# A layer-norm, attention and MLP kernel: a new prologue, transposes by DMA, and logits of two units in three steps from a pool of PSUM banks

## The chip, the cores and the metric

One core of one Trainium2 chip. The metric is the device time of one execution in microseconds (us). Engines: PE multiplies matrices, DVE and ACT do element-wise work and empty PE's results out of PSUM, POOL masks, and SP issues all loads, stores and DMA transposes from one queue, in order. PSUM has eight banks of 128 x 512 float32 values. A matmul writes to a bank, and the bank is free for the next matmul when DVE or ACT has copied the result out (its *eviction*).

## The reference

x is 2048 x 1024. It is normalised to xn. Two branches are computed of xn and added to x.

```python
def _A_ref(x, wq, wk, wv, wo, beta):          # H = 32 heads of Dh = 32, N = 4 segments of L = 512
    q, k, v = ...                             # x @ wq, x @ wk, x @ wv, split into heads and segments
    phi = lambda t: jnp.where(t > 0, t + 1.0, jnp.exp(t))
    for s in range(N):
        p = softmax(qs @ ks.T * scale + causal_mask)
        a_dot = p @ vs
        pq = phi(qs)
        a_mem = (pq @ M) / (pq @ z + 1e-06)
        outs.append(g * a_mem + (1.0 - g) * a_dot)
        pk = phi(ks)
        M = M + pk.T @ vs;  z = z + pk.sum(...)
    return o @ wo

def _B_ref(x, w1, b1, w2, b2):                # w1: 2048 x 3584, w2: 3584 x 2048, mixing over the sequence
    u = gelu(layernorm(x).T @ w1 + b1)
    return (u @ w2 + b2).T

xn = layernorm(x)
return x + _A_ref(xn, ...) + _B_ref(xn, ...)
```

## The kernel before

It has four stages: a *head* (load x, statistics, xn and h, transposes of xn); the *hidden* matmuls h x w1; *attention*, into which the matmuls of w2 and wo (here: *main*) are strewn so that PE has work while others finish; and a short *tail*. Attention goes by *units*. A unit is four heads in one segment; there are 32, eight to a segment. Before the change each job has its fixed banks: logits 0 to 3, the projections 0 to 3 in between, weighing 4 and 5, main 6 and 7 in turn.

```python
LOGIT_STEPS = [[0], [1], [2, 3]]                       # blocks of 128 keys
def logits(self, u, step):                             # banks 0 to 3, one exp for the four
    ...
    fw.op("act", ...activation(self.pT[:, :, off:off + total], self.ps[:, 0:4, 0:total], ACT.Exp, scale=SCALE), ...)

def proj_v(self, m, c, b):                             # values of one 128-row block
    ...                                                # 8 matmuls into bank b
    fw.op("dve", ...tensor_copy(self.vA[i][:, c, :, 0:D_HEAD], self.bank(b)...), ...)

def k_transpose(self, u, b):                           # on PE, then exp (ACT) and phi (DVE)
    for c in range(4):
        fw.tp(bb[:, c * P:(c + 1) * P], self.kT[k][:, c * P:(c + 1) * P], self.ident[:])
    ...
    self.phi(self.pk[j][:]..., self.R_pk[j], bb, self.R_bank[b], 1)

def weigh(self, u, qb):                                # p @ v, phi(q) @ M, and the update of M
    ...                                                # matmuls into bank 4 + qb % 2
    fw.op("dve", ...tensor_copy(dst, self.ps[:, b, 0:n * VW]), ...)            # -> ost
    ...                                                # qb == 3: M update on DVE -> MZ32, MZbf

def combine(self, u):                                  # all on DVE: sums, reciprocal, gate, product, add
    ...
    fw.op("dve", ...tensor_tensor(self.prod[:], ost..., rec..., op=ALU.mult), ...)
    fw.op("dve", ...tensor_tensor(os[:], pv[:, :, 0, :], pv[:, :, 1, :], op=ALU.add), ...)

def main_emit(self, n):                                # n matmuls of main
    ...
    if end == total:                                   # a finished tile: DVE adds it to stg
        fw.op("dve", ...scalar_tensor_tensor(dst, self.bank(b), self.b2c[:, c:c + 1], dst, ...), ...)
        self.main_bank = 13 - b                        # 6, 7, 6, 7, ...

for u in range(N_UNIT):
    n0, n1, n2 = (10, 8, 6) if s == 0 else (11, 9, 9)
    ...
    self.logits(u, 0)
    if u: self.combine(u - 1)
    self.main_emit(n0)
    self.logits(u, 1);  self.main_emit(n1)
    self.logits(u, 2);  self.main_emit(n2)
    self.weigh(u, 0);   self.weigh(u, 1)
    self.proj_q(un, 0)                                 # un = u + 2
    self.o_transpose(u - 1, 2)
    self.k_transpose(u + 1, 3)
    self.weigh(u, 2)
    self.proj_k(un, 1)
    self.weigh(u, 3)
    self.proj_v(m, u % 4, 2)
    self.main_emit(n3)
```

Each engine does its work in the order in which these calls issue it. In the profiles the tiles have the program's names: ps_all is PSUM, qT and kT a unit's queries and keys, pT the logits after exp, vA the values, ost what weighing gives, stg rows of the output to which main is added, w2h a piece of w2, pkT phi(k) before and pk after its transpose.

The softmax here doesn't subtract the row's maximum and nothing guards it: scores larger than these inputs give would overflow.

Of the kernel before, what the change touches and what calls it, by code (L numbers as in the profile page):

```python
# [15 lines left out]
N_SEG = 4  # L16
# [14 lines left out]
PT_OFF = [0, 512, 896, 1152]  # L31
PT_COLS = 1280
# [69 lines left out]
class FW:  # L102
    N_DMA_SEMS = 64
    N_OUT_SEMS = 40
# [94 lines left out]
    def dma(self, out_ap, in_ap, reads=(), writes=(), is_output=False, issuer="sp", extra=(),  # L199
            record_reads=True):  # L200
# [9 lines left out]
        ins = es.eng.dma_start(out_ap, in_ap)  # L210
# [124 lines left out]
class _Kernel:  # L335
    SB_BASE = 16512
    SB_END = 229344
    LEAD = 2
    N_EARLY = 3
# [7 lines left out]
    def build(self):  # L347
        nc, ctx = self.nc, self.ctx
        self.fw = FW(nc, ctx)
        self.x_d = self.A_x[0].rearrange("(c p) d -> p c d", p=P)  # L350
        self.out_d = self.out[0].rearrange("(c p) d -> p c d", p=P)
        self.ps = ctx.enter_context(nc.psum_tensor("ps_all", [P, 8, 512], F32))
        self.R_bank = [Res(f"bank{b}", bank=b) for b in range(8)]
        self.alloc()
        block = ctx.enter_context(nc.Block())

        @block.sync
        def _(sp_eng):
            self.consts()
            self.norm_and_first_hidden()  # L360
            self.over_early()
            self.hidden()
            self.over_late()
            self.attention_and_out()
            self.fw.final_waits()


    def alloc(self):
        nc = self.nc
        a = self.keep = _Arena(nc, self.SB_BASE, self.SB_END)  # L370
        self.ident = a.take("ident", [P, P], BF16)
        self.brow1 = a.take("brow1", [N_FCH, P], BF16)
        self.brow2 = a.take("brow2", [N_TCH, P], BF16)
        self.b1c = a.take("b1c", [P, N_FCH], F32)
        self.b2c = a.take("b2c", [P, N_TCH], F32)
# [7 lines left out]
        self.ln_rs = a.take("ln_rs", [P, N_TCH, 2], F32)  # L383
        self.ln_nb = a.take("ln_nb", [P, N_TCH, 2], F32)
# [5 lines left out]
        self.gT = a.take("gT", [P, N_FCH, D_MODEL], BF16)  # L390

        self.R_ident, self.R_beta, self.R_gcol, self.R_gate = Res("ident"), Res("beta"), Res("gcol"), Res("gate")
        self.R_brow1, self.R_brow2, self.R_b1c, self.R_b2c = Res("brow1"), Res("brow2"), Res("b1c"), Res("b2c")
        self.R_eps, self.R_diag = Res("eps8"), Res("diag")
        self.R_st = [Res(f"st{c}") for c in range(N_TCH)]
        self.R_rs = [Res(f"rs{c}") for c in range(N_TCH)]
        self.R_vA = [[Res(f"vA{i}_{c}") for c in range(4)] for i in range(2)]
# [13 lines left out]
        self.w1ring = [e.take(f"w1s{i}", [P, N_TCH, 256], BF16) for i in range(3)]  # L411
        self.late_end = e.at
        self.R_xin = [Res(f"xin{c}") for c in range(N_TCH)]
        self.R_xnt = [Res(f"xnt{i}") for i in range(4)]
        self.R_h = [Res(f"h{c}") for c in range(N_TCH)]
        self.R_w1s = [Res(f"w1s{i}") for i in range(3)]

    def over_early(self):
# [6 lines left out]
        self.w2r = [e.take(f"w2h{i}", [P, 14, P], BF16) for i in range(4)]  # L425
# [5 lines left out]
        self.R_w2 = [Res(f"w2_{i}", wait) for i in range(4)]  # L431
# [8 lines left out]
        for c in self.mlp_order:  # L440
            for hf in range(2):
                rows = self.B_w2[hf * 14 * P:(hf + 1) * 14 * P, c * P:(c + 1) * P]
                self.w2_ring.srcs.append(rows.rearrange("(fc p) t -> p fc t", p=P))
        for bv in range(2):
            fw.dma(self.wv_sb[:, :, bv * 512:(bv + 1) * 512],
                   self.A_wv[:, bv * 512:(bv + 1) * 512].rearrange("(dc p) j -> p dc j", p=P), writes=[self.R_wv[bv]])
        self.wq_ring.ensure(0)
        self.wk_ring.ensure(0)

    def over_late(self):  # L450
# [5 lines left out]
        self.pk = [e.take(f"pk{i}", [P, 4, P], BF16) for i in range(2)]  # L456
        self.pT = e.take("pT", [P, 4, PT_COLS], BF16)
        self.ost = [e.take(f"ost{i}", [P, 32, VW], BF16) for i in range(2)]
        self.o_s = [e.take(f"o_s{i}", [P, 4, P], BF16) for i in range(2)]
        self.etmp = [e.take(f"etmp{i}", [P, SEG_L], BF16) for i in range(2)]  # L460
        self.mtmp = [e.take(f"mtmp{i}", [P, SEG_L], BF16) for i in range(2)]
# [11 lines left out]
        self.R_pk = [R(f"pk{i}") for i in range(2)]  # L473
        self.R_pTu = [R(f"pTu{k}") for k in range(4)]
        self.R_pTd = [R(f"pTd{k}") for k in range(4)]
        self.R_ost = [[R(f"ost{i}_{qb}") for qb in range(4)] for i in range(2)]
        self.R_os = [R(f"o_s{i}") for i in range(2)]
        self.R_etmp = [R(f"etmp{i}") for i in range(2)]
        self.R_mtmp = [R(f"mtmp{i}") for i in range(2)]
# [11 lines left out]
    def bank_bf(self, b):  # L491
        return self.ps[:, b, :].bitcast(BF16)


    def consts(self):
        fw = self.fw
        self.load_x(0, 1)
        self.load_x(1, 1)
        fw.dma(self.beta_sb[:], self.A_beta.partition_broadcast(P), writes=[self.R_beta])
        self.load_x(2, 2)  # L500
        self.w1_ring = _Ring(fw, [t[:] for t in self.w1ring], self.R_w1s, depth=2)
        for fp in range(N_FCH // 2):
            self.w1_ring.srcs.append(self.B_w1[:, fp * 256:(fp + 1) * 256].rearrange("(c p) f -> p c f", p=P))
        self.w1_ring.depth = 0
        self.w1_ring.ensure(0)
        self.load_x(4, 4)
        fw.dma(self.brow1[:], self.B_b1.rearrange("(c q) -> c q", q=P), writes=[self.R_brow1])
        fw.dma(self.brow2[:], self.B_b2.rearrange("(c q) -> c q", q=P), writes=[self.R_brow2])
        self.w1_ring.ensure(1)
        self.load_x(8, 4)  # L510
        self.load_x(12, 4)
        self.w1_ring.depth = 2

        fw.op("pool", lambda e: e.memset(self.ident[:], 0.0), writes=[self.R_ident])
        fw.op("pool", lambda e: e.affine_select(self.ident[:], self.ident[:], pattern=[[-1, P]],
                                                compare_op=ALU.not_equal, fill=1.0, base=0,
                                                channel_multiplier=1),
              reads=[self.R_ident], writes=[self.R_ident])

        fw.op("act", lambda e: e.activation(self.gcol[:], self.beta_sb[:], ACT.Sigmoid),  # L520
              reads=[self.R_beta], writes=[self.R_gcol])
# [4 lines left out]

    def late_consts(self):
        fw = self.fw
        fw.op("pool", lambda e: e.memset(self.eps8[:, 0, :], 0.0), writes=[self.R_eps])
# [5 lines left out]
        for i in range(2):  # L535
            fw.op("pool", lambda e: e.memset(self.vA[i][:], 1.0), writes=self.R_vA[i])
        gv = self.gcol[:].rearrange("p (g r) -> p g r", r=4)
# [4 lines left out]
        for row, R_row, col, R_col, n, b in ((self.brow1, self.R_brow1, self.b1c, self.R_b1c, N_FCH, 6),  # L542
                                             (self.brow2, self.R_brow2, self.b2c, self.R_b2c, N_TCH, 7)):
            with fw.group(reads=[R_row, self.R_ident], writes=[self.R_bank[b]]):
                fw.tp(self.bank_bf(b)[:, 0:n], row[0:n, :], self.ident[0:n, 0:n])
            fw.op("dve", lambda e: e.tensor_copy(col[:], self.bank_bf(b)[:, 0:n]),
                  reads=[self.R_bank[b]], writes=[R_col])


    def norm_and_first_hidden(self):  # L550
        fw = self.fw
        n_pair = N_TCH // 2
        for p in range(n_pair + 2):
            if p < n_pair:
                self.ln_stats(2 * p)
                self.ln_stats(2 * p + 1)
                self.ln_small(2 * p)
            if 1 <= p <= n_pair:
                self.ln_bias(2 * p - 2)
                for c in (2 * p - 2, 2 * p - 1):  # L560
                    self.ln_apply(c)
            if p == 1:
                self.late_consts()
            if p >= 2:
                for c in (2 * p - 4, 2 * p - 3):
                    self.x_transpose(c)
                    self.early_hidden(c)
            if p == n_pair - 1:
                self.w1_ring.ensure(0)

    def ln_stats(self, c):
        fw = self.fw
        src, st, R = self.xin[:, c, :], self.ln_st[:, c, :], self.R_st[c]
        fw.op("dve", lambda e: e.bn_stats(st[:, 0:6], src[:, 0:512]), reads=[self.R_xin[c]], writes=[R])  # L574
        fw.op("dve", lambda e: e.bn_stats(st[:, 6:12], src[:, 512:1024]), reads=[self.R_xin[c], R], writes=[R])  # L575
        fw.op("dve", lambda e: e.bn_aggr(self.ln_mv[:, c, :], st.rearrange("p (a s) -> p a s", s=6)),  # L576
              reads=[R], writes=[R])

    def ln_small(self, c):

        fw = self.fw
        R, Q = [self.R_st[c], self.R_st[c + 1]], [self.R_rs[c], self.R_rs[c + 1]]
        var, rs = self.ln_mv[:, c:c + 2, 1:2], self.ln_rs[:, c:c + 2, :]
        fw.op("dve", lambda e: e.tensor_scalar(rs[:, :, 0:1], var, LN_EPS, None, op0=ALU.add), reads=R, writes=Q)  # L584
        fw.op("dve", lambda e: e.tensor_scalar(rs[:, :, 1:2], var, 1.0 + LN_EPS, LN_EPS * LN_EPS,
# [167 lines left out]
    def weigh(self, u, qb):  # L753
# [12 lines left out]
        if upd:  # L766
            reads += [self.R_pk[u % 2]]
# [231 lines left out]
```

## Time and profile before

743.61 us is the median of three runs (743.41 to 745.54). The profiled execution took 742.3 us.

| stage, from the timeline of PE; the tail starts at the first matmul of the last output rows | us |
|---|---|
| first hidden matmul | 18.86 |
| head done | 50.5 |
| hidden done | 223.6 |
| first logits | 239.51 |
| one unit in segments 1 and 2 | 16.06 |
| tail starts | 721.33 |
| end | 742.3 |

The page's busy line and its chain of waits (the work that ended last, followed back through what released it):

```profile
span 742.3 us, 11641 instructions
...
PE 707.3 (95%) x5058; PEld 342.0 (46%) x5154; DVE 277.1 (37%) x617; ACT 280.4 (38%) x301; POOL 112.5 (15%) x154
...
PE 91%; DVE 4%; issue 1%; SPq 1%; ACT 1%; DMA 1%; POOL 0%; POOLq 0%; DVEq 0%
```

The waits of PE: on the left what PE was about to write, on the right whose work it waited for; the columns are us in total, times, longest:

```profile
PE ps_all L194 <- DMA brow_50<-in_B_b_dram: 15.0, 1, 15.0
PE ps_all L188 <- issue: 3.8, 11, 2.2
PE ps_all L188 <- DVE pk_1680 L673: 1.7, 1, 1.7
```

PE is the limit nearly everywhere: 95% busy, 91% of the chain. Its only long wait is 15.0 us at the very start, for a load of a bias; the next are 3.8 and 1.7. 50 matmuls of 128x512 take 10.79 us, 0.216 us each.

The timeline of PE over one unit of segment 1; the columns are start, duration, operation, and the number of instructions grouped:

```profile
401.15 0.40 PE L188 MATMUL ps_all<-qT_1673,kT_1676 32*128 32x512 bf16 x4
...
403.96 0.34 PE L188 MATMUL ps_all<-qT_1673,kT_1676 32*128 32x384 bf16 x4
...
406.28 0.34 PE L188 MATMUL ps_all<-qT_1673,kT_1676 32*128 32x256 bf16 x8
...
410.65 0.39 PE L194 MATMUL ps_all<-ident,o_s_1685 128*128 128x128 bf16 x4
410.88 0.39 PE L194 MATMUL ps_all<-ident,kT_1674 128*128 128x128 bf16 x4
...
417.22 0.40 PE L188 MATMUL ps_all<-qT_1671,kT_1674 32*128 32x512 bf16 x4
```

The three logit steps are at 401.15, 403.96 and 406.28, and the next unit's first at 417.22. The two lines of `ident` are the eight transposes on PE. Four of them occupy 0.22 us of the stream (410.655 to 410.878). No row carries an idle time in brackets: the unit has no gap.

### The profile page before, as it was taken

Reading aid. Unit: us, or ns where it says so; the run is one execution under the profiler, and the core shown is the slowest. Engines: PE = TensorE matmul, PEld = TensorE weight load, DVE = VectorE, ACT = ScalarE, POOL = GpSimd, SP = SyncE. Lnnn points to the kernel's source line nnn. Section 1 sums busy time; section 2 is a strip of 40 time slices with the busy share of each in tenths; the row PEclk is TensorE's granted clock in tenths of the full one; section 3 lists DMA queues with packets and bytes.
Section 4 is the critical chain, followed back from the end, with each engine's and each line's share of the span. In section 5 each row is a group of like instructions: output and inputs, shape, how many; then the busy total and the mean of one; then the engine's idle time right before and its main releaser. Section 6 shows DMA issues by size and latency. Waiting matters only on the chain.

```text
span 742.3 us, 11641 instructions
## 1 busy us (share of the span) xinstructions
PE 707.3 (95%) x5058; PEld 342.0 (46%) x5154; DVE 277.1 (37%) x617; ACT 280.4 (38%) x301; POOL 112.5 (15%) x154
## 2 busy tenths in 40 slices
PE   0999999999999999999999999999999999999996
PEld 0444444444444454454444455444455444444452
DVE  6930000000002234335454555554545554444543
ACT  2682121211212443544444343344444344443540
POOL 3640000000000221221121211121211112211220
PEclk9999999999999999999999999999999999999999
DMA  9429322323508141641615415052451606425003
GB/s 253 145 83 218 97 57 82 88 57 91 97 1 223 29 107 29 136 103 34 135 38 100 103 34 135 1 136 55 81 108 29 135 16 120 89 47 108 15 13 115
DMA packets 164603, 65.77 MB, mean 89 GB/s; under 512 B 125642, under 2 KB 156362, under 8 KB 164554
## 3 DMA queue, kind: packets, MB, share of 16 engines
q1 hardware_dynamic: 164554, 65.04, 37.5%
q8 instruction: 40, 0.66, 0.4%
q14 instruction: 9, 0.07, 0.0%
HBM read 59.79 MB, written 5.24 MB: 88 GB/s over the span
## 4 chain that ended last, share of the span: by engine, by line
PE 91%; DVE 4%; issue 1%; SPq 1%; ACT 1%; DMA 1%; POOL 0%; POOLq 0%; DVEq 0%
PE ps_all L188 89%; PE ps_all L194 2%; DVE ln_st L575 1%; SPq L210 1%; DVE ln_st L574 1%; DMA brow_51<-in_B_b_dram 1%; ACT pT L743 0%; DVE ln_mv L576 0%; POOL pT L749 0%; DVE xn_tmp_76 L607 0%; DVE ln_rs L584 0%; DVE fin_8030 L966 0%; DVE fin_8029 L966 0%; ACT xn_tmp_75 L604 0%; DVE xn_tmp_74 L607 0%
## 5 line engine op out<-in xcount | busy, mean ns | idle before, releaser
L743 ACT ACTIVATE pT<-ps_all 128x1536 bf16<-128x1536 f32 (+1 forms) x96 | 152.9, 1593 | 192.9 <-PE ps_all L188 192.9
L749 POOL TENSOR_SCALAR_AFFINE_SELECT pT<-pT 128x512 bf16<-128x512 bf16 x128 | 87.0, 692 | 585.1 <-ACT pT L743 585.1
L662 ACT ACTIVATE gT<-ps_all,b1c 128x512 bf16<-128x512 f32 x56 | 37.8, 689 | 134.5 <-PE ps_all L188 134.5
L710 DVE CAST vA_63<-ps_all 128x512 bf16<-128x512 f32 x16 | 11.1, 694 | 187.9 <-PE ps_all L188 187.7
L188 PE MATMUL ps_all<-h,w1s_79 128*128 128x512 bf16 x311 | 72.0, 382 | 2.7 <-issue 2.2
L188 PE MATMUL ps_all<-h,w1s_80 128*128 128x512 bf16 x314 | 72.3, 381 | 0.3
L188 PE MATMUL ps_all<-h,w1s_81 128*128 128x512 bf16 x251 | 55.6, 379 | 0.3
L188 PE MATMUL ps_all<-gT,w2h_663 128*128 128x512 bf16 x213 | 52.9, 380 | 1.1 <-issue 0.8
L188 PE MATMUL ps_all<-gT,w2h_662 128*128 128x512 bf16 x219 | 53.6, 381 | 0.3
L188 PE MATMUL ps_all<-gT,w2h_665 128*128 128x512 bf16 x214 | 53.0, 380 | 0.9 <-issue 0.6
L188 PE MATMUL ps_all<-gT,w2h_664 128*128 128x512 bf16 x218 | 53.3, 381 | 0.4 <-issue 0.2
L783 DVE CAST ost_1683<-ps_all 128x264 bf16<-128x264 f32 (+1 forms) x64 | 23.7, 391 | 71.8 <-PE ps_all L188 71.8
L783 DVE CAST ost_1684<-ps_all 128x264 bf16<-128x264 f32 (+1 forms) x64 | 23.7, 391 | 68.2 <-PE ps_all L188 68.1
L188 PEld LDWEIGHTS ps_all<-h,w1s_80 128*128 128x128 bf16 x320 | 31.4, 98 | 38.1 <-issue 0.6
L188 PEld LDWEIGHTS ps_all<-h,w1s_79 128*128 128x128 bf16 x320 | 30.7, 98 | 36.8 <-issue 3.0
L188 PEld LDWEIGHTS ps_all<-h,w1s_81 128*128 128x128 bf16 x256 | 25.0, 98 | 30.2
L188 PE MATMUL ps_all<-wo_sb,oT_1691 128*128 128x512 bf16 x126 | 32.4, 379 | 0.2
L188 PEld LDWEIGHTS ps_all<-gT,w2h_665 128*128 128x128 bf16 x224 | 20.6, 98 | 25.2 <-issue 2.5
L188 PEld LDWEIGHTS ps_all<-gT,w2h_663 128*128 128x128 bf16 x224 | 20.6, 98 | 25.2 <-issue 2.5
L188 PE MATMUL ps_all<-wo_sb,xnT_68 128*128 128x512 bf16 x127 | 30.5, 379 | 0.7 <-ACT xnT_68 L835 0.7
L188 PEld LDWEIGHTS ps_all<-gT,w2h_662 128*128 128x128 bf16 x224 | 19.3, 98 | 25.3 <-issue 6.4
L188 PEld LDWEIGHTS ps_all<-gT,w2h_664 128*128 128x128 bf16 x224 | 19.3, 98 | 25.3 <-issue 6.4
(167 smaller groups left out, 870.0 us busy)
## 6 DMA issues: line engine op xcount, KB each, us to landing
w1s_79<-in_B_w_dram SPq DMA_DIRECT2D x5, 1024.0 KB, 5.4
w1s_80<-in_B_w_dram SPq DMA_DIRECT2D x5, 1024.0 KB, 6.0
w1s_81<-in_B_w_dram SPq DMA_DIRECT2D x4, 1024.0 KB, 5.8
wq_658<-in_A_wq_dram SPq DMA_DIRECT2D x16, 256.0 KB, 3.0
wq_659<-in_A_wq_dram SPq DMA_DIRECT2D x16, 256.0 KB, 6.9
wk_660<-in_A_wk_dram SPq DMA_DIRECT2D x16, 256.0 KB, 2.9
wk_661<-in_A_wk_dram SPq DMA_DIRECT2D x16, 256.0 KB, 4.8
w2h_662<-in_B_w_dram SPq DMA_DIRECT2D x8, 448.0 KB, 4.9
```

The lines of the kernel that those rows point to most:

```text
L188: ins = self.nc.tensor.matmul(*args, **kwargs)
L194: ins = self.nc.tensor.transpose(out, in_, ident)
L210: ins = es.eng.dma_start(out_ap, in_ap)
L574: fw.op("dve", lambda e: e.bn_stats(st[:, 0:6], src[:, 0:512]), reads=[self.R_xin[c]], writes=[R])
L575: fw.op("dve", lambda e: e.bn_stats(st[:, 6:12], src[:, 512:1024]), reads=[self.R_xin[c], R], writes=[R])
L662: fw.op("act", lambda e: e.activation(self.gT[:, fc, half * 512:(half + 1) * 512], self.bank(b), ACT.Gelu_apprx_tanh, bias=self.b1c[:, fc: ...
L710: fw.op("dve", lambda e: e.tensor_copy(self.vA[i][:, c, :, 0:D_HEAD], self.bank(b).rearrange("p (h d) -> p h d", d=D_HEAD)), reads=[self.R ...
L743: fw.op("act", lambda e: e.activation(self.pT[:, :, off:off + total], self.ps[:, 0:4, 0:total], ACT.Exp, scale=SCALE), reads=self.R_bank[0:4],
L749: fw.op("pool", lambda e: e.affine_select(d, d, pattern=[[0, 4], [1, P]], compare_op=ALU.is_ge, fill=0.0, base=0, channel_multiplier=-1), ...
L783: fw.op("dve", lambda e: e.tensor_copy(dst, self.ps[:, b, 0:n * VW]), reads=[self.R_bank[b]], writes=[self.R_ost[o][qb]])
```

## The change

The intent was to take work off PE. Three parts:

- a prologue that makes h (which the hidden matmuls need) first, and starts PE with it;
- the transposes of xn, phi(k) and the attention output by DMA, not by PE;
- logits for *pairs* of units in three *windows* of 7, 7 and 6 banks, not in six steps of 4. Every job takes its banks from one pool and gives them back after eviction. Main holds one bank nearly always, so a window of seven needs all the others.

With that the whole order of a pair was written anew. The diff, cut to its core:

```diff
+    def take_bank(self):
+        return self.free.popleft()
+    def give_bank(self, b):
+        self.free.append(b)
...
-    def k_transpose(self, u, b):
-        ...fw.tp(...) on PE...
+    def pk_transpose(self, u):
+        self.fw.dma(self.pk[u % 3][:], self.pkT[:], ..., transpose=True)
...
-    def o_transpose(self, u, b):
-        ...fw.tp(...) on PE, ACT copy...
+    def o_transpose(self, u):
+        self.fw.dma(self.oT[s % 2][:, g, :]..., self.o_s[o][:]..., transpose=True)
...
+    EXPS = ((0, 1, 2, 3, 4, 5, 6), (7, 8, 9, 10, 11, 12, 13), (4, 5, 2, 3, 6, 7))
+    def window(self, p, w):
+        bank = {slot: self.take_bank() for slot in self.EXPS[w]}
+        ...
+        for slot, b in bank.items():
+            fw.op("act", ...activation(pT[:, slot, :], self.bank(b), ACT.Exp, scale=SCALE), ...)
+            self.give_bank(b)
...
+    def settle(self):                     # main is never near the end of its tile at a window
+        left = self.main_left()
+        if 0 < left < 12:
+            self.main_emit(left + 2)
+        elif self.main_at == 0:
+            self.main_emit(2)
...
+        for p in range(N_UNIT // 2):
+            a, b = 2 * p, 2 * p + 1
+            self.settle()
+            self.window(p, 0)
+            self.main_emit(5)
+            self.proj_q(a + 2)            # q copy on ACT, then exp (ACT) and phi (DVE)
+            self.main_emit(4)
+            self.proj_k(a + 2)            # kT cast on DVE, then exp (ACT) and phi (DVE)
+            if p: self.o_transpose(a - 1)
+            self.main_emit(9 if s == 0 else 16)
+            self.pk_transpose(a + 2)
+            self.settle()
+            self.window(p, 1)
+            self.main_emit(5)
+            self.proj_v(a)
+            self.main_emit(5)
+            for qb in range(4): self.weigh(a, qb)
+            self.combine(a)
+            self.main_emit(10 if s == 0 else 17)
+            self.settle()
+            self.window(p, 2)
+            self.o_transpose(a)
+            self.proj_q(b + 2)
+            self.proj_k(b + 2)
+            self.main_emit(4)
+            for qb in range(4): self.weigh(b, qb)
+            self.combine(b)               # before the value projection, and before the next window
+            self.proj_v(b)
+            self.pk_transpose(b + 2)
+            self.main_emit(goal - self.main_done)
```

## The prediction

Written before the changed kernel had run, with its code at hand but no time and no trace of it:

> **What bounds it now.** PE. The page has PE busy 707 of 742 us, and the chain of waits is 91% PE. In the timeline 50 matmuls of 128x512 take 10.79 us: 0.216 us each; there are 2816 (608 us). By stage: first hidden matmul at 18.9 us, head done at 50.5, hidden done at 223.6, units 14.2 us each in segment 0 and 16.06 in segments 1 and 2, last matmul about 735.9, end 742.3.
>
> **What it saves.**
> - Head: h first (stats 1.6 us after the landing at 3.45, h 0.55): PE starts near 6.5 us. Landings and stats gate chunks 1 and 2 (near 12.8); then eight matmuls a chunk, no transposes: done near 37 us with 32 matmuls more. About 20 us.
> - Transposes off PE: 0.22 us per four; 24 of k and 32 of the output: 12 us. The Trainium skill ("VectorE: DVE Perf Modes", The three transpose paths) gives 1309 ns for 128x128 by DMA; no run here shows it yet.
> - Logits: six steps a pair take 2.5 us, about 0.2 us of each switching; three windows about 2.0. 8 us.
> - Tail: eight serial DVE adds (0.6 each) become overlapped: 3 us.
>
> **What it adds: a new wait.** Main holds one bank, so a pair's first window needs all seven others, and PE waits for the eviction of proj_v(b), which stands on DVE behind combine(b), weigh(b)'s four casts, both phis and the kT cast. From the end of window 3, segments 1 and 2, with the trace's durations: ACT does six exps (pitch 0.485) and the q copy to 3.6, exp q to 4.3; DVE phi q to 5.3, kT to 6.0; ACT exp k to 6.7; DVE phi k to 7.7, casts to 9.1, M update to 9.8, combine (0.24+0.38+0.23+1.26+0.5) to 12.4, v cast to 13.1. PE has 20 matmuls, weigh(b) and proj_v: 7.5 us. It waits about 5.7 us. The same sum gives 2 us a pair in segment 0 (short combine, no phi q) and 3.6 in segment 3 with proj_v: about 63 us over 15 boundaries. The second window needs the just finished main bank (eviction 0.75 us, behind two matmuls): 0.6 x 16 = 10 us.
>
> So such a pair takes about 37 us, not 32.1.
>
> **Sum** (estimate): 742 - 20 - 12 - 8 - 3 + 63 + 10 = 772. With DVE idle at the end of proj_k the main wait is still about 3 us, giving about 740. Against that, the skill ("TensorE: Matmul & The Clock Gate", Part 1) says about 3.4 us of idleness can halve PE's clock; this trace agrees at the start (first hidden matmuls about 0.42 us apart, later 0.216).
>
> **Prediction: 766 us, 80% range 726 to 792. Faster by over 2%: 0.14; within 2%: 0.22; slower: 0.64.**
>
> **What would show it.** First hidden matmul near 6.5 us, head done near 37, hidden near 203. No matmuls of ident. Largest of PE's waits: logits behind the DVE cast of vA, 4 to 6 us each in segments 1 and 2; PE busy under 92%. A second, 0.6 us, behind the DVE add of stg. Few waits on transposes.
>
> **What would make it wrong.** A shorter DVE chain; DMA transposes slow enough to hold up the w1, w2, wq, wk loads behind them in the one queue (slower still); a head limited by loading.

## The result, and the profile after

787.56 us is the median of four runs (787.02 to 789.53); the kernel before took 743.53 us beside them. The ratio is 1.059, with a 95% interval of 1.0571 to 1.0608: slower by 6%. (A ratio is the mean time of one kernel's runs over that of the other's runs of the same rounds, so it is not quite the ratio of the medians quoted.) The profiled execution took 787.8 us.

The page's busy line and its chain of waits:

```profile
span 787.8 us, 11445 instructions
...
PE 707.0 (90%) x4728; PEld 333.6 (42%) x4808; DVE 272.4 (35%) x595; ACT 268.4 (34%) x492; POOL 114.0 (14%) x236
...
PE 75%; DVE 14%; ACT 9%; issue 1%; DMA 1%; POOL 0%; SPq 0%; ACTq 0%; POOLq 0%; DVEq 0%
```

The waits of PE:

```profile
PE ps_all L186 <- DVE vA L778: 52.5, 14, 5.0
PE ps_all L186 <- DVE stg L970: 6.6, 16, 0.4
PE ps_all L186 <- POOL pT L832: 6.0, 4, 2.6
...
PE ps_all L186 <- DVE ost L867: 1.6, 1, 1.6
```

PE fell from 95% to 90%, and the chain from 91% PE to 75%, with DVE at 14% and ACT at 9%. The new waits are named: 52.5 us for the DVE cast of vA in 14 places, then 6.6 for stg and 6.0 for POOL's masks. The 15.0 us at the start are gone.

The timeline of PE, the windows of a pair of segment 1; the bracket is the idle time before the row and who ended it:

```profile
414.05 1.00 PE L186 MATMUL ps_all<-qT,kT 32*128 32x512 bf16 x10 [4.97 <-DVE vA L778]
414.98 2.31 PE L186 MATMUL ps_all<-gT,w2h 128*128 128x512 bf16 x5
...
427.18 0.61 PE L186 MATMUL ps_all<-qT,kT 32*128 32x256 bf16 x12 [0.42 <-DVE stg L970]
...
438.79 0.61 PE L186 MATMUL ps_all<-qT,kT 32*128 32x384 bf16 x10
...
452.01 1.03 PE L186 MATMUL ps_all<-qT,kT 32*128 32x512 bf16 x10 [4.96 <-DVE vA L778]
```

Both pairs shown start with 4.96 us of idleness. (Segments 1 and 2 have eight pairs; the first starts with 3.31 us, the other seven with 4.96 to 4.97.) The pair takes 37.96 us (414.05 to 452.01), where two units took 32.13 before. There is a second, quieter loss. The ten logit matmuls behind the gap took 1.00 us and the five main matmuls 2.31. Where no long gap went before, ten take 0.61 (the row at 438.79) and five 1.25: PE comes back at half its rate. The profile has the granted clock (the share of PE's full clock that the chip's throttle let through) at 0.964 over the whole span; it was 1.000 before.

What PE waits for, from the chain of waits of the changed kernel between 400 and 416 us; start, duration, engine and tile:

```profile
401.49 3.04 ACT pT L824 x6
...
405.05 0.64 ACT etmp L717
...
406.04 0.69 DVE pqT L720
406.73 0.61 DVE kT L752
...
407.37 0.64 ACT etmp L717
...
408.36 0.69 DVE pkT L720
409.05 1.36 DVE ost L867 x4
...
411.70 1.24 DVE prod L906
...
412.96 0.42 DVE o_s L910
413.38 0.62 DVE vA L778
...
414.05 1.97 PE ps_all L186 x12
```

This is one string of work, each item waiting for the one above: six exps on ACT, exp of q and k on ACT with phi(q), kT and phi(k) on DVE between them, the four casts of weigh(b), then combine(b), and only then the cast of vA. That cast empties the last of the seven banks which the next window needs.

| stage | before | after | difference |
|---|---|---|---|
| start to first logits | 239.5 | 218.8 | -20.7 |
| attention | 481.8 | 549.3 | +67.5 |
| tail | 21.0 | 19.7 | -1.3 |
| span | 742.3 | 787.8 | +45.5 |

(The changed kernel has done four matmuls of main, 0.9 us, before its first logits; the kernel before has done none.)

So the prologue gave what it promised. Attention lost three times as much.

### The profile page after: what moved, and what is told of

The parts are those of the page before. It is cut to its first block, busy times and chain, and to the rows that moved or that the text cites. A ratio compares the mean times of both kernels' runs of the same rounds, so it can differ in the third digit from the quotient of the medians.

```text
span 787.8 us, 11445 instructions
## 1 busy us (share of the span) xinstructions
PE 707.0 (90%) x4728; PEld 333.6 (42%) x4808; DVE 272.4 (35%) x595; ACT 268.4 (34%) x492; POOL 114.0 (14%) x236
## 2 busy tenths in 40 slices
DMA packets 211181, 77.32 MB, mean 98 GB/s; under 512 B 173754, under 2 KB 203450, under 8 KB 211130
## 4 chain that ended last, share of the span: by engine, by line
PE 75%; DVE 14%; ACT 9%; issue 1%; DMA 1%; POOL 0%; SPq 0%; ACTq 0%; POOLq 0%; DVEq 0%
PE ps_all L186 75%; ACT pT L824 6%; DVE ost L867 2%; ACT etmp L717 2%; DVE prod L906 2%; DVE stg L970 2%; DVE kT L752 1%; DVE vA L778 1%; DVE pqT L720 1%; DVE pkT L720 1%; DVE etmp L718 1%; ACT qT L738 1%; DVE o_s L910 1%; DMA xin<-in_A_x_dram 1%; DVE srec L904 0%
## 5 line engine op out<-in xcount | busy, mean ns | idle before, releaser
L824 ACT ACTIVATE pT<-ps_all 128x512 bf16<-128x512 f32 x320 | 161.8, 619 | 298.5 <-PE ps_all L186 298.5
L186 PE MATMUL ps_all<-gT,w2h 128*128 128x512 bf16 x863 | 220.1, 392 | 1.8 <-issue 0.2
L186 PE MATMUL ps_all<-h,w1all 128*128 128x512 bf16 x878 | 195.7, 383 | 3.8 <-DVE h L603 2.8
L832 POOL TENSOR_SCALAR_AFFINE_SELECT pT<-pT 128x256 bf16<-128x256 bf16 (+3 forms) x176 | 89.0, 510 | 641.4 <-ACT pT L824 636.5
L186 PEld LDWEIGHTS ps_all<-h,w1all 128*128 128x128 bf16 x896 | 88.1, 98 | 111.6 <-issue 7.8
L186 PEld LDWEIGHTS ps_all<-gT,w2h 128*128 128x128 bf16 x896 | 85.8, 100 | 107.1 <-issue 15.7
L186 PE MATMUL ps_all<-qT,kT 32*128 32x128 bf16 (+3 forms) x512 | 32.7, 325 | 60.8 <-DVE vA L778 52.5
L186 PE MATMUL ps_all<-xnT,wq 128*128 128x512 bf16 x256 | 66.6, 407 | 0.0
L186 PE MATMUL ps_all<-xnT,wk 128*128 128x512 bf16 x244 | 59.7, 379 | 0.6
L186 PE MATMUL ps_all<-wv_sb,xnT 128*128 128x512 bf16 x241 | 56.9, 379 | 0.8
L867 DVE CAST ost<-ps_all 128x264 bf16<-128x264 f32 (+1 forms) x128 | 44.1, 391 | 23.1 <-PE ps_all L186 22.9
```

The lines of the kernel that those rows point to most:

```text
L186: ins = self.nc.tensor.matmul(*args, **kwargs)
L824: fw.op("act", lambda e: e.activation(pT[:, slot, :], self.bank(b), ACT.Exp, scale=SCALE), reads=[self.R_bank[b]], writes=[R[slot]])
L832: fw.op("pool", lambda e: e.affine_select(ap, ap, pattern=pat, compare_op=ALU.is_ge, fill=0.0, base=0, channel_multiplier=-1), reads=[R[i] ...
L867: fw.op("dve", lambda e: e.tensor_copy(dst, self.ps[:, b, 0:n * VW]), reads=[self.R_bank[b]], writes=[self.R_ost[o][qb]])
```

## The experiments

All were correct, three rounds each, with the kernel before on the same chip (744.0 to 744.7 us, by batch). Theory A is the one of the prediction: the loss is a wait for a bank, behind a DVE chain that the new order made long. Its rivals: the DMA transposes hold things up, or the windows are slow in themselves. The changed kernel was not run again in these batches; its 787.56 us are from the one before, with a kernel before of 743.53.

### v_first: the value projection before combine(b)

```diff
             for qb in range(4):
                 self.weigh(b, qb)
-            self.combine(b)
             self.proj_v(b)
+            self.combine(b)
             self.pk_transpose(b + 2)
```

> Only the order of two calls changes: proj_v(b) is put before combine(b), so that on DVE the cast of vA no longer stands behind the combine. Theory A (the first window of a pair waits for the last bank, and that bank hangs on the DVE chain): the wait for the cast of vA falls by the length of the combine, about 2.6 us at each boundary of segments 1 to 3 and about 1.2 us in segment 0, from 52.5 us in total to about 20 us; [...]the double-spaced matmuls after them go too (about 15 us). Time about 742 us, between 735 and 758. Rival B (the DMA transposes and the loads queued behind them slow the kernel): the order of two calls changes nothing on the DMA, time 780 to 790. Rival C (the windows of three steps are slow on PE themselves): 780 to 790 as well.

Measured: 746.21 us (744.68 to 746.66), ratio to before 1.0028 (1.0009 to 1.0047). Waits of PE in v_first:

```profile
PE ps_all L186 <- DVE vA L778: 24.6, 14, 2.5
```

Two lines swapped give 41 us back: the vA wait halves, from 4.96 to 2.52 us a pair in segments 1 and 2. 27.9 us (52.5 to 24.6) are the wait. At least 11.5 us of the rest are clock: PE's busy time, with the same matmuls, is 695.5 us where it was 707.0, and the granted clock went from 0.964 to 0.992. The DMA transposes and the windows are the same as in the changed kernel, so neither rival explains more than what is left. The half-rate matmuls did not all go: at the start of a pair they still followed one gap of 2.20 us and one of 2.52.

### prod_twice_b and prod_twice_a: the same extra DVE work in two places

combine() multiplies `prod` a second time, 1.24 us of DVE: in one experiment for the odd units (b), in the other for the even ones (a). The result is unchanged.

```diff
+        if u % 2 == 1:        # prod_twice_b;   u % 2 == 0 in prod_twice_a
+            fw.op("dve", lambda e: e.tensor_tensor(self.prod[:], ost[:, :, 0:D_HEAD], ..., op=ALU.mult), ...)
```

> The multiplication of 128x1024 in combine(b) (second unit of a pair) is done twice with the same result: DVE gets 12 times 1.23 us more. DVE is 35% busy. Theory A: it stands in the chain before the cast of vA, so each of the 10 boundaries after pairs 4 to 13 grows by about 1.26 us: plus 12 to 16 us, about 801 us. Rivals B and C, and the plain reading that an engine that is idle two thirds of the time has room: no change, 786 to 790 us.

> The same doubled multiplication, but in combine(a), the first unit of a pair; the count and the DVE time added are the same. Theory A: the cast of vA is not behind it, and between combine(a) and the next thing that PE waits for on DVE (the eviction of main's bank) PE has over 5 us of matmuls, of which about 1 us is spare: 0 to plus 8 us in all, so clearly less than the other one, most likely under 3 us. If any DVE work costs time, it is as slow as the doubled multiplication in combine(b).

Measured: prod_twice_b 806.46 us (806.14 to 808.84), prod_twice_a 787.0 us (786.5 to 790.34), against 787.56 of the changed kernel. The line of the vA wait, first in prod_twice_b, then in prod_twice_a:

```profile
PE ps_all L186 <- DVE vA L778: 65.2, 14, 6.2
```

```profile
PE ps_all L186 <- DVE vA L778: 52.6, 14, 5.0
```

The same amount of DVE work costs 19 us before the vA cast and nothing elsewhere. The wait grew by 1.26 us a pair in segments 1 and 2 (4.96 to 6.22), which is the added instruction. That is 12.6 of the 19.6 us between the two profiled executions (804.0 and 784.4); the other 7.1 are PE's busy time (715.1 against 708.0), matmuls at half rate after the longer gaps. The expectation, 12 to 16 us, had left these out. DVE's total work is not the limit, only what stands in the queue before that cast.

### tp_twice: every transpose of phi(k) and of the output twice

The second is issued after the first has landed.

```diff
-        self.fw.dma(self.pk[u % 3][:], self.pkT[:], ..., transpose=True)
+        for _ in range(2):
+            self.fw.dma(self.pk[u % 3][:], self.pkT[:], ..., transpose=True)      # and so in o_transpose
```

> Every DMA transpose of phi(k) and of the attention output is issued twice, the second after the first has landed, to the same place: 56 more transposes, 1.2 us of issue each, and the queue stands still for 2.3 to 3.4 us more at each. Theory A: nothing on the critical chain waits for them, time within 1% of 787.6 us (780 to 796). Rival B (they are what costs the time, through the queue): well over that, 815 us or more.

Measured: 801.18 us (799.24 to 802.43), 13.6 over the changed kernel. The expectation was missed; the rival's 815 was not reached either. Waits of PE, then the queue of SP around 220 us (start, duration, operation):

```profile
PE ps_all L186 <- DVE vA L779: 52.6, 14, 5.0
PE ps_all L186 <- DMA w2h<-in_B_w_dram: 7.0, 1, 7.0
```

```profile
219.35 10.04 SPq L208 DMA_TRANSPOSE pk<-pkT  x2
229.43 0.58 SPq L208 DMA_DIRECT2D w2h<-in_B_w_dram  x1
```

The waits at the pairs are unchanged (52.6): the transposes are not what PE waits for there. All the added idleness is *one* wait of 7.0 us where attention starts. Two transposes held SP's queue for 10.04 us, and a load of w2h stood behind them. The profiled execution took 797.1 us, 9.3 over the changed kernel's: the 7.0, and half-rate matmuls after it. The other 4 us of the 13.6 come from which runs were profiled: here the fastest of the four (799.24), of the changed kernel the slowest (789.53). So the rival is wrong about the pairs, but it points to something real, which comes back below: a transpose that can't go yet blocks the loads behind it.

### before_dma_tp: the kernel before, with the DMA transposes alone

Its fixed banks, head and order stay. Only the transposes of phi(k) and of the output move to DMA; phi(k) is then made of kT, right after proj_k. (Not shown in the cut: phi(k) gets a buffer of its own and pk a third one, two temporaries share one, and the numbers of semaphores differ.)

```diff
             if u:
-                self.o_transpose(u - 1, 2)          # PE
-            if u + 1 < N_UNIT and (u + 1) // N_GRP < N_SEG - 1:
-                self.k_transpose(u + 1, 3)          # PE, then exp and phi
+                self.o_transpose(u - 1)             # DMA
             self.weigh(u, 2)
             if un < N_UNIT:
                 self.proj_k(un, 1)
+                self.k_transpose(un)                # exp, phi, then DMA
             self.weigh(u, 3)
             ...
                 self.proj_v(m, u % 4, 2)
```

> What it does: the kernel before, with its fixed banks, its order and its head, and only the transposes of phi(k) and of the attention output moved from the PE to DMA. Theory A (DMA transposes are off the critical path and give back the PE's time): 743.5 less about 12 us of transposes: 731, range 727 to 738. Rival (the DMA transposes cost as much in waits as they save on the PE): 743 or more, with waits of the PE on pkT or oT in the profile.

Measured: 741.58 us (741.09 to 743.26), ratio 0.9968 (0.9953 to 0.9982). Waits of PE:

```profile
PE ps_all L188 <- DVE vA L712: 10.2, 22, 0.8
```

Both were wrong. The transposes left PE, no wait on pkT or oT of note appeared, and yet only 3 us came of it: a unit of segment 1 still took 16.03 us (16.06 before). A *different* wait took the place of the work, 0.35 us at most of the units (10.2 in 22 places), and again it is for the cast of vA. The phi(k) chain on DVE now stood right before it.

### before_dma_tp_v: the same, with phi(k) after the value projection

```diff
                 self.proj_k(un, 1)
-                self.k_transpose(un)
             self.weigh(u, 3)
             ...
                 self.proj_v(m, u % 4, 2)
+            if un < N_UNIT:
+                self.k_transpose(un)
```

> What it does: the experiment before_dma_tp with one line moved: phi(k) of unit u+2 and its transpose are issued after the value projection of the unit instead of before it, so that its DVE work (etmp 0.30, pkT 0.69) doesn't stand before the vA cast. Theory A (before_dma_tp saved its 12 us on the PE and gave 10.2 back as a wait of 0.35 to 0.8 us for vA at 22 unit starts): the wait goes, 731 to 735. Rival (the PE time of the transposes was never worth more than 3 us): 741.

Measured: 729.52 us (728.82 to 729.79), ratio 0.9796 (0.9776 to 0.9815). The time is 1.5 us under the expected range. The vA wait is gone from the profile, and a unit takes 15.61 us. So moving two kinds of transposes off PE is worth 15 us, if what is moved with it doesn't land in front of an eviction that PE waits for. This version, with none of the windows, already beats the kernel before by about 2%.

### deferred: the DVE order of the changed kernel mended

Both phi chains of b + 2 go after the value projection, and combine(b) after the next pair's first window, which is where the kernel before had it.

```diff
             self.window(p, 0)
+            if p:
+                self.combine(a - 1)
 ...
-            self.proj_q(b + 2)
-            self.proj_k(b + 2)
+            self.proj_q(b + 2, later=True)      # without phi
+            self.proj_k(b + 2, later=True)
             self.main_emit(4)
             for qb in range(4):
                 self.weigh(b, qb)
-            self.combine(b)
             self.proj_v(b)
+            self.phi_q(b + 2)
+            self.phi_k(b + 2)
             self.pk_transpose(b + 2)
```

> What it does: only the order of the DVE work changes. In each pair the value projection of the next pair (its cast into vA) is issued before both phi chains, and combine(b) is put off until after the next pair's first window is issued, so that neither stands before the vA cast. Distribution of the main matmuls and the settling wait are as in the changed kernel. Theory A (the wait before a pair's first window is the length of the DVE chain before the vA cast, and the half-speed matmuls after it follow from its length): the chain ends about 0.9 us after the PE is ready in segments 1 and 2, so the vA wait falls from 52 us to under 15, the clock loss of about 18 us goes with it, the 6.6 us behind stg and the 6.0 behind POOL pT stay: 715 to 725 us. Rival (the windows themselves cost the PE, or the DMA transposes do): the order of DVE work is worth no more than v_first found, 744 or more.

Measured: 729.18 us (727.89 to 731.51), ratio 0.98 (0.978 to 0.9821). It is 4 us over the expected range, but the waits are those expected:

```profile
PE ps_all L186 <- DVE vA L788: 11.0, 14, 0.8
PE ps_all L186 <- DVE stg L980: 6.6, 16, 0.4
PE ps_all L186 <- POOL pT L842: 6.0, 4, 2.6
```

The wait before a window is 0.79 us where 0.9 was worked out. The clock is 0.995. Reordering a few DVE instructions thus wins 58 us on the changed kernel: all that the change had lost, and about 2% on the kernel before. The range was too low for its own terms: 787.6 less 41.5 (the vA wait) and less the 18 expected of the clock is 728.

### main_moved, and both: the other remedy, and the two together

Here the DVE order stays, and 16 of a pair's main matmuls are kept back for the place after the value projection, so that PE has 3.4 us of work there. settle() goes.

```diff
-        self.main_emit(4)
-        goal = 0
+        self.main_emit(18)
+        goal = 18
 ...
-            self.settle()                                    # before each window
-            self.main_emit(9 if s == 0 else 16)
+            self.main_emit((7 if s == 0 else 15) if p < 15 else 7)
 ...                                                          # and so on; the last two pairs differ
             self.main_emit(goal - self.main_done)            # 16 matmuls now, before the next window
```

> What it does: the DVE order stays as in the changed kernel; only where the main matmuls are issued changes: 16 of a pair's are kept back and issued after the value projection's matmuls, in front of the next pair's first window, and the settling wait before a pair's second window goes. Theory A: the PE works 16 times 0.216 = 3.4 us while the DVE finishes the chain, so the vA wait falls from 4.96 to about 1.6 us in segments 1 and 2 and to none in segment 0; a gap of 1.6 us costs no clock; the 6.6 us behind stg and most of the 6.0 behind POOL pT go: 712 to 725 us. Rival (the DVE is the limit of a pair, not the place of its work): the wait moves elsewhere and the time stays over 740.

> What it does: the DVE order of the one and the main distribution of the other experiment together. Theory A: no wait of the PE longer than 1 us at any pair's start; the PE is packed from its first matmul to the tail: 218.8 us to the first window, 462 us of attention matmuls, about 19 us of tail: 700 us, range 696 to 708. PE busy 98% or more. Rival (the DVE, ACT or the exps are nearly as full as the PE and a new wait appears): 715 or more, with a new named wait of over 10 us.

Measured: main_moved 745.93 us (743.78 to 747.93), ratio 1.0031; both 736.51 us (731.9 to 737.37), ratio 0.9883. Both missed their ranges by over 20 us. Waits of PE, first in main_moved, then in both:

```profile
PE ps_all L186 <- DMA w2h<-in_B_w_dram: 24.7, 15, 2.5
```

```profile
PE ps_all L186 <- DMA w2h<-in_B_w_dram: 21.7, 14, 4.5
```

The vA wait is gone (in main_moved 1.6 us a pair had been expected to stay), and in its place stands a wait for the *loads* of w2h. The timeline of both around 444 us (start, duration, engine, operation) shows how it comes about there:

```profile
442.69 0.69 DVE L720 SCALAR_TENSOR_TENSOR pkT<-kT,etmp 128x512 bf16<-128x512 bf16 x1
...
443.41 1.20 SPq L208 DMA_TRANSPOSE pk<-pkT  x1
...
444.65 1.78 SPq L208 DMA_DIRECT2D w2h<-in_B_w_dram  x3
...
445.01 0.82 PE L186 MATMUL ps_all<-gT,w2h 128*128 128x512 bf16 x3
...
447.58 0.60 PE L186 MATMUL ps_all<-gT,w2h 128*128 128x512 bf16 x2 [1.75 <-DMA w2h<-in_B_w_dram]
```

phi(k) ends on DVE at 443.38. SP has the transpose of pkT at the front of its queue and waits for that; three loads of w2h stand behind it and are issued at 444.65, and PE, which used up what it had, waits for them until 447.58. With the kept-back matmuls PE uses more of w2h just there. Ten of the 14 waits of both, 16.2 of the 21.7 us, follow such a transpose that SP stood waiting to issue; the largest, 4.5 us, is at the start of attention, behind a transpose that took 2.5 us to issue; three of 0.3 to 0.4 us follow a store.

In main_moved it is not the transpose. The front of the queue is a store of finished output there, in the timeline around 441 us:

```profile
440.37 0.74 DVE L970 SCALAR_TENSOR_TENSOR stg<-ps_all,bc,stg 128x512 bf16<-128x512 f32 x1
...
441.14 0.36 SPq L208 DMA_DIRECT2D out_dram<-stg  x1
...
442.01 0.46 SPq L208 DMA_DIRECT2D w2h<-in_B_w_dram  x1
```

The store waits for DVE's add into stg, which stands in the long DVE chain, behind phi(k). SP stood still for 6.8 us until that add ended at 441.11; the load behind the store came at 442.01, and PE waited for it until 445.21. All 15 waits of main_moved follow such a store, for which SP had stood still for 4.7 to 6.8 us. The rivals of both experiments came true in their numbers (over 740 us with the wait moved elsewhere; a new named wait of over 10 us), but not in their reason: PE waits for loads, though in main_moved they are late through DVE's chain, and both2 below shows that neither DVE nor ACT is the limit of a pair.

### both2 and main_moved_w2: the loads in front of the transpose, and further ahead

```diff
-        self.w2_ring.ensure(0)
+        self.w2_ring.ensure(3)                               # fill all six slots before attention
 ...
                 w, R_w = self.w2_ring.get(4 * j + at // 7)
+                if half:                                     # second use of these weights: slots come free
+                    self.w2_ring.ensure(4 * j + at // 7 + 2)
 ...
             self.proj_v(b)
+            self.main_emit(goal - self.main_done)
             self.phi_q(b + 2)
             self.phi_k(b + 2)
             self.pk_transpose(b + 2)
-            self.main_emit(goal - self.main_done)
```

main_moved_w2 has no separate phi calls and moves the transpose alone. both2 also keeps back 10 matmuls at the start where both has 18, so that no tile of main ends just before a window in segment 0. main_moved_w2 has main_moved's order on DVE and its 18.

> What it does: the experiment both, with its w2h wait taken away by three edits: the loads of w2h run up to two chunks further ahead in the second half of each output tile (whose slots are free by then) and all six slots are filled before the attention starts; the two phi chains and the pk transpose that follows them in the in-order SP queue are issued after the trailing main matmuls and their loads; eight of the kept-back matmuls fewer are carried across, so that a main tile's end falls away from the windows of segment 0. Theory A (all that was left in both was w2h queued on SP behind a transpose that waits for phi, 21.7 us, and stg 6.6 us in segment 0): 736 less 28 and less the clock behind them: 703, range 698 to 712, PE waiting for nothing longer than 1 us after the head. Rival (loads are limited by DMA bandwidth with the transposes on it, not by their place in the queue): the w2h wait stays over 10 us and the time over 720.

> What it does: the experiment main_moved, whose DVE order is that of the changed kernel, with the w2h loads further ahead and before the pk transpose in the SP queue, as in both2. Theory A: the w2h wait of 24.7 us goes, a vA wait of about 1.6 us per pair (17 us in all) or less comes into sight in its place in segments 1 and 2, the stg waits of segment 0 (6.8) stay: 742 less 10 to 25: 718 to 732. Rival (a chain of DVE work as long as a pair): over 738 with the whole of the vA wait back.

Measured: both2 705.14 us (704.66 to 706.09), ratio 0.9474 (0.945 to 0.9497); main_moved_w2 731.53 us (730.96 to 733.4), ratio 0.9828 (0.9805 to 0.9852). Page lines and waits of PE in both2:

```profile
span 703.0 us, 11460 instructions
...
PE 686.8 (98%) x4728; PEld 326.9 (47%) x4808; DVE 274.8 (39%) x595; ACT 267.4 (38%) x492; POOL 114.3 (16%) x236
```

```profile
PE ps_all L186 <- ACT pT L834: 2.5, 15, 0.2
PE ps_all L186 <- DVE h L603: 2.1, 1, 2.1
```

The w2h wait is gone in both kernels. A lack of DMA bandwidth, the rival of both2, was thus not the cause: the same 77.32 MB are moved in less time. Two remedies were put in together, the place of the transpose and the loading ahead; which of them was needed was not tested. In main_moved the transpose had not been in the way, so there it was most likely the loading ahead: in main_moved_w2 SP still stands still before the stores, for 4.7 to 6.8 us, and PE waits for no load. In main_moved_w2 the vA wait is back at 16.9 us, 2.2 at most, as expected for a DVE chain that is covered and not shortened. In both2 nothing is left after the head but 0.2 us a pair and 0.4 once, for a mask of POOL: PE is 98% busy, and a pair of segment 1 takes 31.13 us. This version beats both kernels, the one before by 5.3% (0.9474) and the changed one by some 10% (705.14 against 787.56, of different batches).

| kernel | median us | largest named waits of PE, us in total | clock |
|---|---|---|---|
| before | 743.6 | brow 15.0 (head) | 1.000 |
| changed | 787.6 | vA 52.5 | 0.964 |
| v_first | 746.2 | vA 24.6 | 0.992 |
| prod_twice_b | 806.5 | vA 65.2 | 0.953 |
| prod_twice_a | 787.0 | vA 52.6 | 0.969 |
| tp_twice | 801.2 | vA 52.6, w2h 7.0 | 0.962 |
| deferred | 729.2 | vA 11.0 | 0.995 |
| main_moved | 745.9 | w2h 24.7 | 0.988 |
| main_moved_w2 | 731.5 | vA 16.9 | 0.989 |
| both | 736.5 | w2h 21.7 | 0.991 |
| both2 | 705.1 | ACT pT 2.5 | 0.998 |
| before_dma_tp | 741.6 | brow 15.0, vA 10.2 | 0.999 |
| before_dma_tp_v | 729.5 | brow 14.8 | 0.998 |

## Why the prediction was right or wrong

The direction and the mechanism were right. 787.6 us is within the range of 726 to 792, though 22 us above the 766 predicted.

**The main wait: right, sized a little too high.** The prediction named the cast of vA, the bank it holds and the items before it. The chain in the trace has the same items in the same order. Predicted 5.7 us a pair in segments 1 and 2, 2 in segment 0, 3.6 in segment 3; measured 4.96 (3.31 at the first of them), 1.70, and 3.07 to 3.24. The prediction had the chain 13.1 us long after window 3; it was 12.5. In sum 63 us predicted, and 54.1 measured (vA 52.5, and ost 1.6 at the last pair). v_first and the two prod_twice runs show it as cause, not only as company.

**The second wait: right, too high.** 0.6 us 16 times predicted, 0.42 measured: 10 against 6.6 us.

**Not foreseen: POOL.** The last two pairs have no projections left, and PE waits 6.0 us for masks. In sum the three waits are 66.7 us, where 73 were predicted.

**The step that failed: the clock was named, and left out of the sum.** The prediction cites the Trainium skill ("TensorE: Matmul & The Clock Gate", Part 1), that about 3.4 us of idleness can halve PE's clock, beside its own wait of 5.7 us, and then adds no term for it. All seven gaps of 4.96 us came before matmuls at half rate. What that cost can be read from busy and idle time, since both2 has the same matmuls in another order:

| profiled execution | PE busy | PE idle | span |
|---|---|---|---|
| before | 707.3 | 35.0 | 742.3 |
| changed | 707.0 | 80.8 | 787.8 |
| both2 | 686.8 | 16.2 | 703.0 |

The change did remove 20.5 us of work from PE (707.3 to 686.8), and half-rate matmuls put 20.2 us back. So busy time stood still, and the whole loss seems to be idleness. (Ends of matmuls are modelled, and 80 to 96 matmul records are missing from each of the three traces, so these are good to a few us.) A count of the slow matmuls in the traces agrees. Against both2 the changed kernel has 79 more 128x512 matmuls at half rate, 0.21 us longer each, and eight windows that took about 1.0 us and not 0.61: 17 and 3 us. A sum that began at 772 and got 20.2 for the clock and -6.3 for the waits comes to 786; the rest of the terms nearly cancel.

**The head: right.** First hidden matmul at 6.81 (6.5 predicted), first four tiles evicted from 36.97 (37), hidden done at 204.04 (203). 20.7 us won up to the first logits, 20 predicted. That is the stage from one trace to the other; the prologue was not run alone, and 2.6 of the 20.7 are there in before_dma_tp_v too (first logits at 236.87). The prologue also starts PE with eight matmuls on zeros, from 1.25 us; what these are worth was not tested, and 14 hidden matmuls from 7.9 us on still ran at half rate.

**The transposes: the size about right, the place not examined.** 12 us predicted; before_dma_tp_v won 15. But before_dma_tp shows that this is not a matter of PE's time alone: on the kernel before the same move won 3 us until the phi chain was taken out from before the cast. The DMA transposes themselves never appear among PE's named waits of the changed kernel. They do matter through SP's queue (tp_twice, both).

**The windows: about 4 us at most shown, 8 predicted.** From first logits to tail it is 464.96 us in both2 and 470.9 in before_dma_tp_v, which has fixed banks and steps by unit: 5.9 less, but 2.2 of that are ten matmuls of main that both2 does before its first logits. The two differ in more than the windows, so this is a difference of two packed schedules and not a test of windows alone.

**The tail: 3 us predicted, 1.3 measured.** Its parts were not tested.

## What to carry to other kernels

When a step takes nearly all of a pool of buffers, look up which eviction gives back the *last* buffer and count everything that its engine does before it, in queue order; put into that stretch only what the next step needs (here: the cast before combine and phi, 58 us for a few lines). Price a gap with what comes after it too: here half-rate matmuls cost 20 us on top of 67 us of waiting. And whatever is put into an in-order queue of loads must be ready when it gets there, or the loads behind it wait as well.

## What the Trainium skill lacked or had wrong

- "TensorE: Matmul & The Clock Gate", Part 1 gives about 3.4 us as the idle window after which the clock is halved. Here shorter gaps did it at times. Over all traces, counting gaps in PE's stream after the head which a 128x512 matmul follows within 1 us: 0 of 52 gaps of 1.0 to 2.0 us, 11 of 25 of 2.0 to 2.7 us (the shortest 2.12), 8 of 14 of 2.7 to 3.4 us, and all 33 of 4.3 to 7.0 us were followed by half-rate matmuls. To read it as "safe below 3.4 us" would be wrong. No lone gap below 2 us did it; but in six kernels two gaps near the end, 2.6 and 1.1 us with 0.3 us of matmuls between, were followed by half-rate matmuls each time. The page's remark that the window is free-running fits with equal gaps going either way (2.52 us in v_first: one of seven). Its spacing of 215.7 ns for warm 512-column matmuls agrees with the 0.216 us here.
- "VectorE: DVE Perf Modes", The three transpose paths gives 390 ns on TensorE and 1309 ns by DMA for 128x128. In a packed stream a PE transpose took 0.056 us here (four in 0.22). A DMA transpose of 128x512 took 2.3 us (phi(k)) to 3.4 us (output) from issue to landing, and 1.2 us of SP's queue to issue, where loads of 224 and 256 KB mostly took 0.43 to 0.58. The section has neither the stream figure nor the queue time, and it was these two that mattered here.
- "DMA: Bandwidth & Descriptors", Issuing engines are not separate DMA queues says that the sequencer time of issuing is usually small. The section does not say what the order of an issuing queue can cost. Here a transpose or a store that waited for its data held up the loads behind it, and PE waited for loads 21.7 us in both (mostly behind transposes), 24.7 us in main_moved (behind stores) and 7.0 us in tp_twice, with that queue's packets at 41 to 42% of the DMA engines' time in the first two, and at 43.7% in both2, where the wait is gone.
